# Long convolution and soft mixture of experts on one core: the second transform stage on four frequencies at once, one in each quarter of the matrix array

## The chip, the cores and the metric

The kernel runs on one core of a Trainium2 chip. The metric is device time in microseconds (us) from the first to the last instruction, the median of several runs. Every program here runs on one core. PE is TensorE's matrix array, DVE is VectorE, ACT is ScalarE, POOL is GpSimd, SP is the engine that issues the transfers.

## The reference

A causal convolution along the sequence, written as a Fourier transform of twice the length, and then a soft mixture of experts over all 45,568 rows:

```python
B, S, D = 8, 5696, 128
Xf = rfft(x, n=2*S, axis=1); Hf = rfft(h, n=2*S, axis=0)
y  = irfft(Xf * Hf, n=2*S, axis=1)[:, :S, :]
x  = y.reshape(B*S, D)
logits = x @ phi                               # phi: 128 x 32 slots
d = softmax over rows of logits;  slot_input = d.T @ x
slot_out = per expert: relu(slot_input @ w1) @ w2
out = softmax over slots of logits @ slot_out  # 45568 x 128, float32
```

## The kernel before

The transform is done in two stages, over 90 and over 64 points. Per batch (and once for the filter `h`, called batch 0) there are eight steps. Stage A does the 90-point transform and writes to HBM. Stage B reads 128 rows for a *unit* of two frequencies in each of two halves (23 units a batch): b1 is the 64-point transform, VectorE multiplies by the filter's spectrum, b2 transforms back. Stage C takes the result, folds it, makes the logits and the softmax sums. The three stages run interleaved, each for another batch: step 9 starts B for the filter, step 17 B for the first batch, step 26 starts C; stage A ends with step 71, B with step 80. A step has three *slots* of stage B, and each slot holds b1 of unit u and b2 of unit u-1.

```python
wt = fconst.tile([P, NP, P], F32, name="wt")     # NP = 45 tables of 128 x 128, block-diagonal
vt = fconst.tile([P, NP, P], F32, name="vt")
ps  = mid.enter_context(tc.tile_pool(name="ps", bufs=6, space=PSUM))   # bank() takes from here
aps = mid.enter_context(tc.tile_pool(name="aps", bufs=2, space=PSUM))

def stage_b1(u):
    g, i = divmod(u, NU); n = min(2, NP - 2 * i)
    t_ = gs.pop(u)
    p = bank()
    pv = p[:, :].rearrange("p (q c d) -> p q c d", c=2, d=D)
    for q in range(n):
        nc.tensor.matmul(p[:, q * 256:(q + 1) * 256], wt[:, 2 * i + q, :],
                         t_[:, q, :, :].rearrange("p c d -> p (c d)"), start=True, stop=True)
    # ... g == 0: the filter's spectrum Hr, Hi is made from pv; return
    for t, H in ((pr, Hr), (pi, Hi)):            # DVE, out of PSUM
        nc.vector.tensor_tensor(out=t[:, 0:n, :, :], in0=pv[:, 0:n, :, :], in1=H[...], op=AL.mult)
    # ... DVE: yf = pr[0] - pi[1], pr[1] + pi[0]; prods[u] = yf

def stage_b2(u):
    # ...
    p = bank()
    for q in range(n):
        nc.tensor.matmul(p[:, q * 256:(q + 1) * 256], vt[:, 2 * i + q, :], y_[:, q, :, :]..., ...)
    nc.scalar.activation(st[:, 0:n, :], p[:, 0:n * 256]..., AF.Copy)   # zst, then to HBM

def slot_b():
    if us:
        u = us.pop(0); prefetch(u + AHEAD)
        stage_b1(u); wait_b2.append(u)
        if len(wait_b2) > 1: stage_b2(wait_b2.pop(0))
    elif wait_b2: stage_b2(wait_b2.pop(0))

# one step t (C works on pairs of steps):
#   stage_a(t, 0); [odd: dispatch]; slot_b(); [even: C1, C4]; [odd: C2 transposes, C6]; slot_b()
#   [even: fold_out, C5]; stage_a(t, 1); [odd: C3 = logits and their maximum mx]; slot_b(); ...
```

Everything is float32: a matmul becomes two matrix instructions (the trace has 810 for the 405 matmuls of b1). The tile layer makes all waits from the program's order, and for PSUM it orders any two accesses to one bank of one tile in which one engine writes.

## Time and profile before

| | before |
|---|---|
| time, median of 4 runs | 1061.7 us |
| profiled run | 1066.3 us |
| busy share PE, DVE, ACT, POOL | 91, 68, 48, 34% |
| start of steps 17, 26; of C's pairs 23 and 27 (steps 72 and 80) | 111, 196; 804, 894 us |
| eight steps in the steady part (steps 34 to 66) | 104.9 us |

Starts of steps are those of stage A's first matmul of the step in the trace. How its lines are read is shown in the prediction. The short way: the slices say where PE is full, the chain of waits says which engine's instructions stand one behind the other up to the end, and the groups give for each line the count, the mean duration and what ended the idle time before it.

### The profile page before, as it was taken

Reading aid. Unit: us, or ns where it says so; the run is one execution under the profiler, and the core shown is the slowest. Engines: PE = TensorE matmul, PEld = TensorE weight load, DVE = VectorE, ACT = ScalarE, POOL = GpSimd, SP = SyncE. Lnnn points to the kernel's source line nnn. Section 1 sums busy time; section 2 is a strip of 40 time slices with the busy share of each in tenths; the row PEclk is TensorE's granted clock in tenths of the full one; section 3 lists DMA queues with packets and bytes.
Section 4 is the critical chain, followed back from the end, with each engine's and each line's share of the span. In section 5 each row is a group of like instructions: output and inputs, shape, how many; then the busy total and the mean of one; then the engine's idle time right before and its main releaser. Section 6 shows DMA issues by size and latency. Waiting matters only on the chain.

```text
span 1066.3 us, 17253 instructions
## 1 busy us (share of the span) xinstructions
PE 968.4 (91%) x5690; PEld 606.3 (57%) x5690; DVE 723.7 (68%) x1384; ACT 517.1 (48%) x1049; POOL 358.5 (34%) x340
## 2 busy tenths in 40 slices
PE   6688899999999999999999999999998998775983
PEld 2255566555666666666666566656665555343683
DVE  2044566677777787777777777777778888565442
ACT  3467444455555555555555555555553434343342
POOL 5523222323433343334333333343321212384000
PEclk9899999999999999999999999999999999886855
DMA  6999999988888889888988898889877777953398
GB/s 193 288 277 289 304 333 283 296 257 258 245 274 260 265 236 282 263 257 244 279 254 270 238 276 265 259 241 278 285 214 245 247 229 214 242 158 156 135 406 340
DMA packets 175111, 275.50 MB, mean 258 GB/s; under 512 B 12864, under 2 KB 115776, under 8 KB 169263
## 3 DMA queue, kind: packets, MB, share of 16 engines
q1 hardware_dynamic: 174447, 274.04, 82.8%
q8 instruction: 47, 0.77, 0.3%
q10 hardware_dynamic: 576, 0.36, 0.1%
q14 instruction: 41, 0.34, 0.1%
HBM read 145.95 MB, written 128.39 MB: 257 GB/s over the span
## 4 chain that ended last, share of the span: by engine, by line
PE 64%; DVE 21%; DMA 8%; issue 2%; ACT 2%; POOL 1%; SPq 0%; DVEq 0%; ACTq 0%; POOLq 0%
PE bank L190 18%; PE bank L220 12%; PE bank L308 11%; PE bank L256 11%; DVE yf L242 5%; DMA out_dram<-o 4%; PE bank L338 3%; DVE pr L238 3%; DMA gt<-f 3%; DVE pi L238 3%; PE bank L348 2%; DVE y L325 2%; DVE y L324 2%; PE bank L377 2%; DVE yf L244 2%
## 5 line engine op out<-in xcount | busy, mean ns | idle before, releaser
L179 POOL TENSOR_TENSOR x<-xc 128x512 f32<-128x512 f32 x144 | 187.5, 1303 | 281.9 <-PE bank L190 237.0
L190 PE MATMUL bank<-x,s 128*128 128x512 f32 x576 | 270.6, 597 | 8.1 <-POOL x L179 8.1
L259 ACT ACTIVATE zst<-bank 128x512 f32<-128x512 f32 (+1 forms) x184 | 108.2, 588 | 296.3 <-PE bank L256 280.6
L220 PE MATMUL bank<-gt,wt 128*128 128x256 f32 x810 | 220.4, 395 | 20.1 <-DMA gt<-f 19.8
L220 PEld LDWEIGHTS bank<-gt,wt 128*128 128x128 f32 x810 | 145.4, 192 | 115.1 <-issue 54.3
L256 PE MATMUL bank<-yf,vt 128*128 128x256 f32 x720 | 189.4, 385 | 17.7 <-DVE yf L244 12.5
L192 ACT ACTIVATE fst<-bank 128x512 f32<-128x512 f32 x288 | 168.5, 598 | 67.7 <-PE bank L190 53.1
L238 DVE TENSOR_TENSOR pr<-bank,Hr 128x512 f32<-128x512 f32 (+1 forms) x184 | 124.6, 677 | 97.8 <-PE bank L220 97.7
L256 PEld LDWEIGHTS bank<-yf,vt 128*128 128x128 f32 x720 | 133.5, 190 | 53.0 <-issue 13.8
L190 PEld LDWEIGHTS bank<-x,s 128*128 128x128 f32 x576 | 107.5, 192 | 94.6 <-issue 61.8
L308 PE MATMUL bank<-zc,i 128*64 128x512 f32 x480 | 120.3, 612 | 3.5 <-DMA zc<-z 3.5
L238 DVE TENSOR_TENSOR pi<-bank,Hi 128x512 f32<-128x512 f32 (+1 forms) x184 | 123.0, 668 | 0.0
L242 DVE TENSOR_TENSOR yf<-pr,pi 128x256 f32<-128x256 f32 (+1 forms) x184 | 113.5, 617 | 6.4
L338 PE MATMUL bank<-ident,y 128*128 128x128 f32 x512 | 67.2, 289 | 15.3 <-DVE y L325 15.3
L358 DVE TENSOR_REDUCE mx<-lt 64x1 f32<-64x360 f32 x64 | 33.2, 518 | 70.1 <-ACT lt L352 69.7
L244 DVE TENSOR_TENSOR yf<-pr,pi 128x256 f32<-128x256 f32 (+1 forms) x184 | 76.5, 416 | 0.0
L338 PEld LDWEIGHTS bank<-ident,y 128*128 128x128 f32 x512 | 62.2, 150 | 20.6 <-issue 16.5
L339 ACT ACTIVATE yt<-bank 128x360 f32<-128x360 f32 x128 | 56.4, 471 | 35.6 <-PE bank L338 35.6
L229 DVE SCALAR_TENSOR_TENSOR Hr<-bank,turn,pr 128x128 f32<-128x128 f32 x45 | 15.7, 348 | 75.6 <-ACT pr L227 75.6
L324 POOL TENSOR_TENSOR y<-y,op 128x512 f32<-128x512 f32 x32 | 38.4, 1200 | 80.9 <-DVE op L313 80.9
L308 PEld LDWEIGHTS bank<-zc,i 128*64 128x64 f32 x480 | 30.1, 137 | 56.3 <-issue 53.9
L413 POOL TENSOR_TENSOR L<-L,rs 128x512 f32<-128x512 f32 x32 | 33.6, 1051 | 77.8 <-DVE rs L412 64.7
(97 smaller groups left out, 922.2 us busy)
## 6 DMA issues: line engine op xcount, KB each, us to landing
f<-fst SPq DMA_DIRECT2D x144, 360.0 KB
gt<-f SPq DMA_DIRECT2D x198, 256.0 KB
z<-zst SPq DMA_DIRECT2D x176, 256.0 KB
zc<-z SPq DMA_DIRECT2D x60, 720.0 KB
xc<-in_x_dram SPq DMA_DIRECT2D x64, 320.0 KB
out_dram<-o SPq DMA_DIRECT2D x16, 1024.0 KB
out_dram<-o SPq DMA_DIRECT2D x8, 768.0 KB
c_t<-cst SPq DMA_DIRECT2D x26, 180.0 KB
```

What stands on the lines that cost most here:

```text
L179: nc.gpsimd.tensor_tensor(out=y_[:, :, :], in0=t_[:, 0, :, :], in1=t_[:, 1, ::-1, :], op=AL.subtract if comp else AL.add)
L190: nc.tensor.matmul(p[:, :], s1[:, tab[G], :], src[:, :, :].rearrange("p n d -> p (n d)"), start=True, stop=True)
L192: nc.scalar.activation(st[:, :, G, :], p[:, :].rearrange("p (n d) -> p n d", d=D), AF.Copy)
L220: nc.tensor.matmul(p[:, q * 256:(q + 1) * 256], wt[:, 2 * i + q, :], t_[:, q, :, :].rearrange("p c d -> p (c d)"), start=True, stop=True)
L238: nc.vector.tensor_tensor(out=t[:, 0:n, :, :], in0=pv[:, 0:n, :, :], in1=H[:, 2 * i:2 * i + n, :].unsqueeze(2).broadcast_to([P, n, 2, D]), ...
L242: nc.vector.tensor_tensor(out=y_[:, 0:n, 0, :], in0=pr[:, 0:n, 0, :], in1=pi[:, 0:n, 1, :], op=AL.subtract)
L244: nc.vector.tensor_tensor(out=y_[:, 0:n, 1, :], in0=pr[:, 0:n, 1, :], in1=pi[:, 0:n, 0, :], op=AL.add)
L256: nc.tensor.matmul(p[:, q * 256:(q + 1) * 256], vt[:, 2 * i + q, :], y_[:, q, :, :].rearrange("p c d -> p (c d)"), start=True, stop=True)
L259: nc.scalar.activation(st[:, 0:n, :], p[:, 0:n * 256].rearrange("p (q c) -> p q c", q=n), AF.Copy)
L308: nc.tensor.matmul(p[h_ * HP:(h_ + 1) * HP, :], i1[:, tab, :], t_[:, o, :, q, :], start=True, stop=True)
L324: eng.tensor_tensor(out=part(v, 1), in0=part(v, 0), in1=o_[:, :, :], op=AL.subtract)
L338: nc.tensor.transpose(p[:, i * P:(i + 1) * P], ys[T][:, k * CH + i, 0:D], ident[:, :])
```

## The change

The tables `wt` and `vt` held two 64 x 64 blocks on the diagonal of a 128 x 128 block, the rest zeros. The change stores the 64 x 64 blocks alone and lets four frequencies use the four quarters of the array at once: the row half is the half of the frequencies for b1, the column half is the frequency's parity; b2 goes the other way. The change has the instructions of different row halves write to different banks, so a unit's output is spread over two banks. To use no more than the eight banks of the kernel before (6 + 2), b1 of unit u and b2 of unit u-1 share one tile of two banks: b1 has columns 0 to 255 of both, b2 columns 256 to 511. Stage A's write to HBM is split in two, as its rows now lie in two groups of partitions.

```diff
-    ps = mid.enter_context(tc.tile_pool(name="ps", bufs=6, space=PSUM))
-    aps = mid.enter_context(tc.tile_pool(name="aps", bufs=2, space=PSUM))
+    rings = [mid.enter_context(tc.tile_pool(name="ps", bufs=4, space=PSUM))]
+    bps = front.enter_context(tc.tile_pool(name="bps", bufs=2, space=PSUM))
-    wt = fconst.tile([P, NP, P], F32, name="wt")
-    vt = fconst.tile([P, NP, P], F32, name="vt")
+    wt = fconst.tile([P, NP, HP], F32, name="wt")
+    vt = fconst.tile([P, NU, 2, HP], F32, name="vt")
 ...
-        p = bank()
-        for q in range(n):
-            nc.tensor.matmul(p[:, q * 256:(q + 1) * 256], wt[:, 2 * i + q, :], ...)
+        for a in range(2):
+            r = slice(a * HP, (a + 1) * HP)
+            for q in range(n):
+                nc.tensor.matmul(bt[q * HP:(q + 1) * HP, a, 0:2 * D], wt[r, 2 * i + q, :],
+                                 t_[r, q, :, :].rearrange("p c d -> p (c d)"), ...)
 ...
-        p = bank()
         for q in range(n):
-            nc.tensor.matmul(p[:, q * 256:(q + 1) * 256], vt[:, 2 * i + q, :], ...)
+            r = slice(q * HP, (q + 1) * HP)
+            for a in range(2):
+                nc.tensor.matmul(bt[a * HP:(a + 1) * HP, q, 2 * D:4 * D], vt[r, i, a, :], ...)
 ...
         def slot_b():
+            bt = bps.tile([P, 2, 512], F32, name="bt", tag="bt")
+            fresh = bool(us)
+            if fresh:
                 u = us.pop(0)
                 prefetch(u + AHEAD)
-                stage_b1(u)
+                stage_b1(u, bt)
                 wait_b2.append(u)
-                if len(wait_b2) > 1:
-                    stage_b2(wait_b2.pop(0))
+            if len(wait_b2) > fresh:
+                stage_b2(wait_b2.pop(0), bt)
```

(Cut: the tables, the filter's branch, the split write, the loads, the early return of `slot_b` when nothing is left to do, and the branch of `slot_b` that this replaces. The layouts of the data follow. P is 128, HP 64, D 128, NP 45, NU 23.)

More of the change, by code (lines that the diff above doesn't have):

```diff
@@ L15, with transform_tables @@
 PSUM = bass.MemoryType.PSUM
-def transform_tables(S, N1, N2, CH, Z0, X0, F0):
+def transform_tables(S, N1, N2, CH, Z0, X0, F0, F1):
     N, R1, HALF, P = N1 * N2, S // N2, N2 // 2, 2 * N2
@@ L36, in transform_tables @@
     i1 = np.stack([np.cos(a0), -np.sin(a0), -np.cos(a0)], 1)
-    s1 = np.pad(s1, [(X0, P - R1 - X0), (0, 0), (F0, P - N1 - F0)])
+    NP = N1 // 2
+    part = s1
+    s1 = np.zeros((P, 3, P))
+    for a, p in enumerate((F0, F1)):
+        s1[X0:X0 + R1, :, p:p + NP] = part[:, :, a * NP:(a + 1) * NP]
     i1 = np.pad(i1[np.arange(N1).reshape(2, N1 // 2).T.reshape(-1)],
@@ L44, in transform_tables @@
     w = np.concatenate([np.cos(a2), np.sin(a2)], 1)
-    NP = N1 // 2
     back = np.arange(N2).reshape(2, HALF // CH, CH).transpose(1, 0, 2).reshape(-1)
-    wbd = np.zeros((2 * N2, NP, 2 * N2))
-    vbd = np.zeros((2 * N2, NP, 2 * N2))
-    for par in range(2):
-        r = slice(par * N2, (par + 1) * N2)
-        wbd[par::2, :, r] = w[par * NP:(par + 1) * NP].transpose(1, 0, 2)
-        vbd[r, :, r] = w[par * NP:(par + 1) * NP][:, back].transpose(2, 0, 1)
-    turn = (N1 - 1) / 2 * alpha[:, None] + (N2 - 1) / 2 * omega
-    tn = np.zeros((2 * N2, 2, NP))
-    for par in range(2):
-        r = slice(par * N2, (par + 1) * N2)
-        tn[r, 0] = np.cos(turn[par * NP:(par + 1) * NP]).T / N
-        tn[r, 1] = np.sin(turn[par * NP:(par + 1) * NP]).T / N
-    return [np.ascontiguousarray(t, dtype=np.float32) for t in (s1, i1, wbd, vbd, tn)]
+    NU = (NP + 1) // 2
+    turn = (N1 - 1) / 2 * alpha[:, None] + (N2 - 1) / 2 * omega
+    wq = np.zeros((2, N2, NP, N2))
+    vq = np.zeros((2, N2, NU, 2, N2))
+    tn = np.zeros((2, N2, 2, NU, 2))
+    for a in range(2):
+        wq[a] = w[a * NP:(a + 1) * NP].transpose(1, 0, 2)
+        for q in range(NP):
+            vq[q % 2, :, q // 2, a] = w[a * NP + q][back].T
+            tn[q % 2, :, 0, q // 2, a] = np.cos(turn[a * NP + q]) / N
+            tn[q % 2, :, 1, q // 2, a] = np.sin(turn[a * NP + q]) / N
+    wq, vq, tn = [t.reshape(P, *t.shape[2:]) for t in (wq, vq, tn)]
+    return [np.ascontiguousarray(t, dtype=np.float32) for t in (s1, i1, wq, vq, tn)]
 @with_exitstack
@@ L106 @@
     SPLIT = R1 // 16 * 16
-    Z0, X0, F0 = 20, 20, 19
+    Z0, X0, F0, F1 = 20, 20, 6, 82
     ctx.enter_context(tc.manual_schedule())
@@ L111 @@
         nc.inline_tensor(t, f"tab_{n}").ap()
-        for n, t in zip(("s1", "i1", "w", "v", "turn"), transform_tables(S, N1, N2, CH, Z0, X0, F0))]
-    fd = [nc.dram_tensor(f"f_{g}", (N2, N1, 2, D), F32, kind="Internal").ap() for g in range(B + 1)]
+        for n, t in zip(("s1", "i1", "w", "v", "turn"), transform_tables(S, N1, N2, CH, Z0, X0, F0, F1))]
+    fd = [nc.dram_tensor(f"f_{g}", (2, N2, NP, 2, D), F32, kind="Internal").ap() for g in range(B + 1)]
     zd = [nc.dram_tensor(f"z_{b}", (NP, 2 * N2, 2, D), F32, kind="Internal").ap() for b in range(B)]
@@ L130 @@
     ypool = work.enter_context(tc.tile_pool(name="ypool", bufs=1))
+    front = ExitStack()
     mid, inner, cload = ExitStack(), ExitStack(), ExitStack()
-    ps = mid.enter_context(tc.tile_pool(name="ps", bufs=6, space=PSUM))
-    aps = mid.enter_context(tc.tile_pool(name="aps", bufs=2, space=PSUM))
-    front = ExitStack()
+    rings = [mid.enter_context(tc.tile_pool(name="ps", bufs=4, space=PSUM))]
+    bps = front.enter_context(tc.tile_pool(name="bps", bufs=2, space=PSUM))
     fconst = front.enter_context(tc.tile_pool(name="fconst", bufs=1))
@@ L140 @@
     s1 = apool.tile([P, 3, P], F32, name="s1", tag="s1", bufs=1)
-    wt = fconst.tile([P, NP, P], F32, name="wt")
-    vt = fconst.tile([P, NP, P], F32, name="vt")
-    turn = fconst.tile([P, 2, NP], F32, name="turn")
-    Hr = fconst.tile([P, NP, D], F32, name="Hr")
-    Hi = fconst.tile([P, NP, D], F32, name="Hi")
+    wt = fconst.tile([P, NP, HP], F32, name="wt")
+    vt = fconst.tile([P, NU, 2, HP], F32, name="vt")
+    turn = fconst.tile([P, 2, NU, 2], F32, name="turn")
+    Hr = fconst.tile([P, NU, 2, D], F32, name="Hr")
+    Hi = fconst.tile([P, NU, 2, D], F32, name="Hi")
     def bank():
-        return ps.tile([P, 512], F32, name="bank", tag="bank")
+        rings.append(rings.pop(0))
+        return rings[-1].tile([P, 512], F32, name="bank", tag="bank")
     xs = {}
@@ L194, in stage_a @@
         n0 = comp * HALF + CH * j
-        nc.sync.dma_start(out=fd[g][n0:n0 + CH, :, :, :].rearrange("n k g d -> k n (g d)"),
-                          in_=st[F0:F0 + N1, :, :, :].rearrange("k n g d -> k n (g d)"))
+        for a, p in enumerate((F0, F1)):
+            nc.sync.dma_start(
+                out=fd[g][a, n0:n0 + CH, :, :, :].rearrange("n q c d -> q n (c d)"),
+                in_=st[p:p + NP, :, :, :].rearrange("k n c d -> k n (c d)"))
     gs, prods = {}, {}
@@ L208, in load_g, with stage_b1 @@
             out=t_[:, 0:n, :, :].rearrange("p q c d -> p (q c d)"),
-            in_=fd[g].rearrange("r (a p) c d -> (r a) (p c d)",
-                                a=2)[:, 4 * i * D:(4 * i + 2 * n) * D])
+            in_=fd[g].rearrange("a r q c d -> (a r) (q c d)")[:, 4 * i * D:(4 * i + 2 * n) * D])
         gs[u] = t_
-    def stage_b1(u):
+    def stage_b1(u, bt):
         g, i = divmod(u, NU)
@@ L216, in stage_b1 @@
         t_ = gs.pop(u)
-        p = bank()
-        pv = p[:, :].rearrange("p (q c d) -> p q c d", c=2, d=D)
-        for q in range(n):
-            nc.tensor.matmul(p[:, q * 256:(q + 1) * 256], wt[:, 2 * i + q, :],
-                             t_[:, q, :, :].rearrange("p c d -> p (c d)"), start=True, stop=True)
+        for a in range(2):
+            r = slice(a * HP, (a + 1) * HP)
+            for q in range(n):
+                nc.tensor.matmul(bt[q * HP:(q + 1) * HP, a, 0:2 * D], wt[r, 2 * i + q, :],
+                                 t_[r, q, :, :].rearrange("p c d -> p (c d)"),
+                                 start=True, stop=True)
+        r = slice(0, n * HP)
+        pv = bt[r, :, 0:2 * D].rearrange("p a (c d) -> p a c d", c=2)
         if g == 0:
-            for q in range(n):
-                m = 2 * i + q
+            for a in range(2):
                 pr = bpool.tile([P, 2, D], F32, name="pr", tag="pr")
                 for c in range(2):
-                    nc.scalar.activation(pr[:, c, :], pv[:, q, c, :], AF.Copy,
-                                         scale=turn[:, 0, m:m + 1])
+                    nc.scalar.activation(pr[r, c, :], pv[:, a, c, :], AF.Copy,
+                                         scale=turn[r, 0, i, a:a + 1])
                 nc.vector.scalar_tensor_tensor(
-                    out=Hr[:, m, :], in0=pv[:, q, 1, :], scalar=turn[:, 1, m:m + 1],
-                    in1=pr[:, 0, :], op0=AL.mult, op1=AL.add)
+                    out=Hr[r, i, a, :], in0=pv[:, a, 1, :], scalar=turn[r, 1, i, a:a + 1],
+                    in1=pr[r, 0, :], op0=AL.mult, op1=AL.add)
                 nc.vector.scalar_tensor_tensor(
-                    out=Hi[:, m, :], in0=pv[:, q, 0, :], scalar=turn[:, 1, m:m + 1],
-                    in1=pr[:, 1, :], op0=AL.mult, op1=AL.subtract, reverse1=True)
+                    out=Hi[r, i, a, :], in0=pv[:, a, 0, :], scalar=turn[r, 1, i, a:a + 1],
+                    in1=pr[r, 1, :], op0=AL.mult, op1=AL.subtract, reverse1=True)
             return
@@ L238, in stage_b1, with stage_b2 @@
             nc.vector.tensor_tensor(
-                out=t[:, 0:n, :, :], in0=pv[:, 0:n, :, :],
-                in1=H[:, 2 * i:2 * i + n, :].unsqueeze(2).broadcast_to([P, n, 2, D]), op=AL.mult)
+                out=t[r, :, :, :], in0=pv,
+                in1=H[r, i, :, :].unsqueeze(2).broadcast_to([n * HP, 2, 2, D]), op=AL.mult)
         y_ = bpool.tile([P, 2, 2, D], F32, name="yf", tag="yf")
-        nc.vector.tensor_tensor(out=y_[:, 0:n, 0, :], in0=pr[:, 0:n, 0, :], in1=pi[:, 0:n, 1, :],
+        nc.vector.tensor_tensor(out=y_[r, :, 0, :], in0=pr[r, :, 0, :], in1=pi[r, :, 1, :],
                                 op=AL.subtract)
-        nc.vector.tensor_tensor(out=y_[:, 0:n, 1, :], in0=pr[:, 0:n, 1, :], in1=pi[:, 0:n, 0, :],
+        nc.vector.tensor_tensor(out=y_[r, :, 1, :], in0=pr[r, :, 1, :], in1=pi[r, :, 0, :],
                                 op=AL.add)
         prods[u] = y_
-    def stage_b2(u):
+    def stage_b2(u, bt):
         g, i = divmod(u, NU)
@@ L253, in stage_b2 @@
         y_ = prods.pop(u)
-        p = bank()
         for q in range(n):
-            nc.tensor.matmul(p[:, q * 256:(q + 1) * 256], vt[:, 2 * i + q, :],
-                             y_[:, q, :, :].rearrange("p c d -> p (c d)"), start=True, stop=True)
+            r = slice(q * HP, (q + 1) * HP)
+            for a in range(2):
+                nc.tensor.matmul(bt[a * HP:(a + 1) * HP, q, 2 * D:4 * D], vt[r, i, a, :],
+                                 y_[r, a, :, :].rearrange("p c d -> p (c d)"),
+                                 start=True, stop=True)
         st = bpool.tile([P, 2, 2 * D], F32, name="zst", tag="zst", bufs=3)
-        nc.scalar.activation(st[:, 0:n, :], p[:, 0:n * 256].rearrange("p (q c) -> p q c", q=n),
-                             AF.Copy)
+        nc.scalar.activation(st[:, 0:n, :], bt[:, 0:n, 2 * D:4 * D], AF.Copy)
         nc.sync.dma_start(
@@ L417, in dispatch @@
     def dispatch(T):
-        ap_ = aps.tile([P, 512], F32, name="ap", tag="ap")
+        ap_ = bank()
         d_ = ds.pop(T)
@@ L541, in slot_b @@
         def slot_b():
-            if us:
+            if not us and not wait_b2:
+                return
+            bt = bps.tile([P, 2, 512], F32, name="bt", tag="bt")
+            fresh = bool(us)
+            if fresh:
                 u = us.pop(0)
                 prefetch(u + AHEAD)
-                stage_b1(u)
+                stage_b1(u, bt)
                 wait_b2.append(u)
-                if len(wait_b2) > 1:
-                    stage_b2(wait_b2.pop(0))
-            elif wait_b2:
-                stage_b2(wait_b2.pop(0))
-        for tab, src, first in ((wt, t_w, LAG_B - 2), (vt, t_v, LAG_B + NJ - 2)):
-            p0 = 2 * PER * (t - first)
-            if 0 <= p0 < NP:
-                p1 = min(NP, p0 + 2 * PER)
-                nc.sync.dma_start(out=tab[:, p0:p1, :], in_=src[:, p0:p1, :])
+            if len(wait_b2) > fresh:
+                stage_b2(wait_b2.pop(0), bt)
+        for tab, src, first, n, k in ((wt, t_w, LAG_B - 2, NP, 2 * PER),
+                                      (vt, t_v, LAG_B + NJ - 2, NU, PER)):
+            p0 = k * (t - first)
+            if 0 <= p0 < n:
+                v = slice(p0, min(n, p0 + k))
+                nc.sync.dma_start(out=tab[:, v], in_=src[:, v])
         if pair(1 - 2 * ahead) is not None:
@@ L603 @@
             front.close()
+            rings.append(mid.enter_context(tc.tile_pool(name="ps2", bufs=4, space=PSUM)))
             last = work.enter_context(tc.tile_pool(name="last", bufs=1))
@@ L677 @@
                 out=hidT[:, g, k0:k0 + 4, :], in_=p[:, :].rearrange("p (k c) -> p k c", k=4))
-    sop = aps.tile([P, 512], F32, name="ap", tag="ap")
+    sop = bank()
     for g in range(EG):
```

## The prediction

> **What bounds the kernel now.** I read the page first: busy times, slices, chain of waits, groups.
>
> ```profile
> PE 968.4 (91%) x5690; PEld 606.3 (57%) x5690; DVE 723.7 (68%) x1384; ACT 517.1 (48%) x1049; POOL 358.5 (34%) x340
> ...
> PEclk9899999999999999999999999999999999886855
> DMA  6999999988888889888988898889877777953398
> ...
> PE 64%; DVE 21%; DMA 8%; issue 2%; ACT 2%; POOL 1%; SPq 0%; DVEq 0%; ACTq 0%; POOLq 0%
> ...
> L220 PE MATMUL bank<-gt,wt 128*128 128x256 f32 x810 | 220.4, 395 | 20.1 <-DMA gt<-f 19.8
> ...
> L256 PE MATMUL bank<-yf,vt 128*128 128x256 f32 x720 | 189.4, 385 | 17.7 <-DVE yf L244 12.5
> ```
>
> The matrix engine leads and owns the chain. L220 (first half of stage two, "b1") and L256 (second half, "b2") are 24% of the chain. Next I asked for busy time by stretches of 100 us (columns: PE, PEld, DVE, ACT, POOL, clock, DMA share, GB/s).
>
> ```profile
> 300.00:400.00 100.00, 99.54 (x560) 61.93 (x559) 79.52 (x148) 53.07 (x103) 38.20 (x35) 1.00 0.87 261
> 800.00:900.00 100.00, 88.99 (x555) 55.82 (x555) 83.45 (x169) 40.84 (x82) 19.80 (x22) 1.00 0.75 236
> ```
>
> From 200 to 800 us PE has no free time (99.5%); VectorE at 79% and DMA at 87% are close behind. Then I read single slots in the order of time; a slot is one b1 and the previous unit's b2.
>
> ```profile
> 161.95 1.03 PE L220 MATMUL bank<-gt,wt 128*128 128x256 f32 x4
> ...
> 162.81 1.03 PE L256 MATMUL bank<-yf,vt 128*128 128x256 f32 x4
> 163.02 0.69 DVE L238 TENSOR_TENSOR pr<-bank,Hr 128x512 f32<-128x512 f32 x1 [1.36 <-PE bank L220]
> ...
> 163.62 0.68 DVE L238 TENSOR_TENSOR pi<-bank,Hi 128x512 f32<-128x512 f32 x1
> 163.68 1.03 PE L220 MATMUL bank<-gt,wt 128*128 128x256 f32 x4
> ```
>
> b1 issues for 0.86 us (161.95 to 162.81), b2 for 0.87 (to 163.68): 1.72 us a slot, four 128x256 matrix instructions of 0.214 us each per half. The 1.03 includes a 0.17 us tail that overlaps the next. The point to see: b2 starts at 162.81, **before** VectorE begins pr on b1's result, because they use different banks.
>
> **What the Trainium skill says.** "TensorEngine Tiling (Array Packing)", Key Properties: tiles run in parallel, and changing the tiling mode drains the engine. The trace agrees: eight 128x32 instructions of 360 columns (L348) go from 403.04 to 403.85 in the timeline, against 8 x 0.30 = 2.4 us one after another, so four run at once; going from L256 to the two-tile L308 takes 0.96 us start to start where 0.85 is work, so a switch costs some 0.11. "PSUM — Partial Sum Buffer", PSUM bank collisions raise a hardware error: two engines must not touch one bank and quadrant at once, disjoint columns or not. Nothing in the trace of before shows this; the changed program's waits do. "TensorE: Matmul & The Clock Gate", Part 1: the matrix clock is halved after an idle window of about 3.4 us. The trace agrees and is stricter; these are single windows:
>
> ```profile
> 105.18:108.59 3.41, 1.77 (x7) 0.76 (x5) 1.46 (x5) 2.67 (x9) 1.27 (x1) 1.00 0.84 244
> 112.01:115.42 3.41, 1.47 (x6) 0.68 (x4) 0.31 (x2) 1.62 (x4) 1.59 (x2) 1.00 1.02 335
> 115.42:118.83 3.41, 3.15 (x8) 1.91 (x7) 2.71 (x6) 0.00 (x0) 0.00 (x0) 0.50 1.03 329
> ```
>
> A window with 1.77 us busy left the clock alone; one with 1.47 us (1.94 us idle) was followed by a window at 0.50. So idle of some 1.9 us within one window costs a half-speed window.
>
> **The change part by part.**
>
> Removed: each full unit had 2 x 4 instructions over the whole array. It now has 2 x 8 on quarters, four at once: two rounds of 0.214 = 0.43 us per half. Taken alone, a slot goes from 1.72 to 0.86 us. There are 207 b1 and 184 b2, so some 160 us of PE time is removed. The tables halve (2.9 MB less of 275 MB).
>
> Added, small: stage one's write is split in two (144 issues more, same bytes, 1 KB pieces as before); the mode changes before b1 and after b2, 0.11 us each, 0.22 per slot, of which 4 of 12 per two steps were paid already; the general ring of banks is 4 rather than 6 plus 2.
>
> Added, large: b1(u) and b2(u-1) now share one two-bank tile, b1 in columns 0 to 255 of both banks and b2 in 256 to 511. In program order VectorE's pr(u) and pi(u) stand between them. I resolved the waits of the built program: in before, the first matmul of b2 waits for yf of the *previous* unit and an old bank; in after, it waits for pi of *this* unit, every slot. So the order becomes b1, pr, pi, b2, with PE idle between. From the slot above: b1's issue ends at 162.81; tail and signal 0.21 until pr starts (163.02); pr and pi 1.28 (until 164.30); from VectorE's end to the first matmul of b2 0.14 (yf ends 846.83, L256 starts 846.97). Gap 0.21 + 1.28 + 0.14 = 1.63 us.
>
> New slot: 0.43 + 1.63 + 0.43 + 0.22 = 2.71 us against 1.72: **+0.99**. Not hidden, as PE is in order and had no free time.
>
> One slot in six is worse. In odd steps the reduction mx and its followers come before the third slot's pr in VectorE's order:
>
> ```profile
> 404.43 1.05 DVE L358 TENSOR_REDUCE mx<-lt 64x1 f32<-64x360 f32 x2 [1.78 <-ACT lt L352]
> 405.51 0.16 DVE L363 SCALAR_TENSOR_TENSOR low<-mx,low 128x1 f32<-128x1 f32 x1
> 405.71 0.16 DVE L366 TENSOR_TENSOR df<-low 128x1 f32<-128x1 f32 x1
> 405.78 0.68 DVE L238 TENSOR_TENSOR pr<-bank,Hr 128x512 f32<-128x512 f32 x1
> ```
>
> They take 1.35 us and begin 1.39 after the logits matmul's start (403.04); b1's result would be ready 1.35 after it. So this slot waits 1.4 us more. The other slots' VectorE backlog fits in PE's work between slots, while stage one runs.
>
> The sum by stretches (steps 17 to 25, A and B alone, at 116 to 200 us; steps 26 to 71, all stages, to 803 us; steps 72 to 80 without stage one, to 905 us):
> - Until 116 us: PE waits for DMA there; smaller tables: -4.
> - Steps 17 to 25: 26 slots x 0.99 = 26, less 5 of idle time that it had: +20.
> - Steps 26 to 71: eight steps take 104.84 us now (L308 in the chain at 304.38 and 409.22). Added per eight: 23 x 0.99 = 22.8, - 1.8 for switches paid already, + 4 x 1.4 = 5.6: 26.6. Times 46/8: +153.
> - Steps 72 to 80: VectorE bound, some 22.7 us per two steps; the new serial chain is 8.6 (other PE work) + 0.5 + 6 x 2.6 + 2.7 of backlog = 27.4: +20.
> - Clock: the slot behind mx leaves PE idle about 2.8 us, more than 1.9; wherever the windows fall, some 70% of these 23 slots start one or two half-speed windows, each costing 1.5 us: about +40, and +15 in the stretches where slots stand next to each other.
> - After 905 us: nothing.
>
> 1062 - 4 + 20 + 153 + 20 + 55 = **1306 us**.
>
> **The rivals.**
> 1. *The packing pays.* If b2 didn't wait, PE would need 160 - 35 us less, VectorE (82 us per 105) and DMA (91 per 105) would bind instead, and it would end near 980. For: PE at 99.5%. Against: the wait is in the program, for every unit that has a b2.
> 2. *The quarters do not overlap four ways* with these row and column halves: 0.43 us more per half, up to +160, near 1440. Against: four row strips (L716) and four column strips (L348) each overlapped fully.
> 3. *The clock stays up*, as matmuls are still busy 70% of the time: near 1250.
> 4. *The ring of 4 banks or the doubled writes bind.* The queue has only eight transfers in flight, but each step gets longer, so its load falls; I give these nothing.
>
> **Range and chances.** 1250 without the clock, 1306 with my guess, up to 1385 if many windows run at half speed; an overestimated gap gives 1225. Range 1225 to 1385. Faster 0.03, same 0.02, slower 0.95.
>
> **What would show it right or wrong.** Right: b2's row of waits names VectorE's pi, some 180 times and 1.4 us or more each (250 us in all); PE's busy share falls from 91% to about 65 to 70%; ACT's zst comes right behind each pi; clock below 1.00 in 200 to 800 us; DMA share falls below 0.75. Each half takes 0.43 + 0.17 us as a group of eight. Wrong: b2 starting before pi ends, which would mean rival 1; b1 taking 0.86 for eight, rival 2; clock 1.00 throughout, rival 3.

## The result

| | before | after |
|---|---|---|
| time, median | 1061.7 us | 1300.1 us |
| range, 4 runs each | 1060.0 to 1063.7 | 1296.5 to 1305.4 |
| ratio | | 1.225 (95%: 1.220 to 1.230) |
| busy share of PE, DVE | 91, 68% | 72, 54% |
| mean matrix clock | 0.953 | 0.911 |
| eight steps in the steady part | 104.9 us | 136.2 us |

A ratio is the mean time of one kernel's runs over that of the other's of the same rounds, so it is not quite the ratio of the medians. The changed kernel is 22% slower.

The page of the changed kernel, the lines that answer to those of before (busy times; the clock and DMA rows of the 40 slices; the chain of waits by engine; the two halves of stage B, now lines 266 and 227):

```profile
PE 937.9 (72%) x7220; PEld 418.2 (32%) x7220; DVE 701.3 (54%) x1386; ACT 522.6 (40%) x1051; POOL 355.4 (27%) x340
...
PEclk9898997998999899989999899999999788888775
DMA  7888777776677667766677767667665566477199
...
PE 61%; DVE 25%; DMA 7%; issue 2%; ACT 2%; SPq 1%; POOL 0%; DVEq 0%; ACTq 0%; POOLq 0%
...
L266 PE MATMUL bt<-yf,vt 64*64 64x256 f32 x1440 | 133.8, 437 | 289.3 <-DVE pi L247 289.3
...
L227 PE MATMUL bt<-gt,wt 64*64 64x256 f32 x1620 | 142.6, 418 | 21.2 <-DMA gt<-f 9.9
```

The two halves of stage B did become shorter: 134 + 143 us busy, from 189 + 220. But L266 carries 289 us of idle PE time ahead of it, all of it ended by VectorE's pi. PE's own list of waits has it as one row (us in total, times, longest):

```profile
PE bt L266 <- DVE pi L247: 289.3, 176, 3.0
```

One slot of the changed kernel in the order of time, PE and VectorE:

```profile
502.35 0.66 PE L227 MATMUL bt<-gt,wt 64*64 64x256 f32 x8
...
503.08 0.69 DVE L247 TENSOR_TENSOR pr<-bt,Hr 128x512 f32<-128x512 f32 x1 [4.03 <-PE bt L227]
503.69 0.68 DVE L247 TENSOR_TENSOR pi<-bt,Hi 128x512 f32<-128x512 f32 x1
...
504.40 0.43 DVE L251 TENSOR_TENSOR yf<-pr,pi 128x256 f32<-128x256 f32 x1
...
504.42 0.66 PE L266 MATMUL bt<-yf,vt 64*64 64x256 f32 x8 [1.41 <-DVE pi L247]
```

Eight instructions of b1 take 0.66 us as a group, tail included: four quarters do run at once. Then PE stands still until pi has ended (504.37). Before, b2 began ahead of pr. What b2 reads is the *previous* unit's yf, which was ready long before; the yf at 504.40 is for the next slot. So b2 waits for no data: it waits because pi reads the bank that b2 is about to write.

The third slot of an odd step, where the logits' maximum mx stands ahead of pr on VectorE:

```profile
529.49 0.81 PE L358 MATMUL bank<-yt,phi 128*32 128x360 f32 x8
...
530.23 0.66 PE L227 MATMUL bt<-gt,wt 64*64 64x256 f32 x8
...
530.88 1.05 DVE L368 TENSOR_REDUCE mx<-lt 64x1 f32<-64x360 f32 x2 [3.16 <-ACT lt L362]
...
532.24 0.69 DVE L247 TENSOR_TENSOR pr<-bt,Hr 128x512 f32<-128x512 f32 x1
...
533.57 0.66 PE L266 MATMUL bt<-yf,vt 64*64 64x256 f32 x8 [2.68 <-DVE pi L247]
```

From b1 to b2 3.34 us, against 2.07 in the slot above. Two single windows (us, then busy PE, PEld, DVE, ACT, POOL, clock, DMA share, GB/s) show what such a gap does to the clock:

```profile
494.73:498.14 3.41, 0.90 (x13) 0.21 (x8) 2.45 (x6) 0.67 (x2) 0.98 (x1) 1.00 0.98 259
498.14:501.56 3.42, 3.26 (x11) 1.47 (x12) 0.87 (x3) 0.68 (x2) 0.00 (x0) 0.50 0.94 312
```

PE was busy for 0.90 us of the first, and the next one ran at half speed. Summed over the trace, the clock stood at one half for 74 us between steps 26 and 71, against none before.

Where the 237 us (profiled runs) came from: 1.5 until step 17, 32 in steps 17 to 25, 178 in steps 26 to 71, 29 from the start of step 72 to the start of step 80, and -3 after that.

### The profile page after: what moved, and what is told of

It is laid out like the page before. It is cut to its first block, busy times and chain, and to the rows that moved or that the text cites. A ratio compares the mean times of both kernels' runs of the same rounds, so it can differ in the third digit from the quotient of the medians.

```text
span 1303.6 us, 20188 instructions
## 1 busy us (share of the span) xinstructions
PE 937.9 (72%) x7220; PEld 418.2 (32%) x7220; DVE 701.3 (54%) x1386; ACT 522.6 (40%) x1051; POOL 355.4 (27%) x340
## 4 chain that ended last, share of the span: by engine, by line
PE 61%; DVE 25%; DMA 7%; issue 2%; ACT 2%; SPq 1%; POOL 0%; DVEq 0%; ACTq 0%; POOLq 0%
PE bank L196 20%; PE bt L266 10%; PE bank L318 9%; DVE pr L247 9%; DVE pi L247 8%; PE bt L227 8%; PE bank L348 5%; DMA out_dram<-o 3%; DVE mx L368 2%; PE bank L434 2%; PE bank L358 2%; DMA gt<-f 1%; PE bank L387 1%; ACT lt L362 1%; PE bank L410 1%
## 5 line engine op out<-in xcount | busy, mean ns | idle before, releaser
L266 PE MATMUL bt<-yf,vt 64*64 64x256 f32 x1440 | 133.8, 437 | 289.3 <-DVE pi L247 289.3
L196 PE MATMUL bank<-x,s 128*128 128x512 f32 x576 | 315.7, 679 | 10.2 <-DMA xc<-in_h_dram 8.3
L270 ACT ACTIVATE zst<-bt 128x512 f32<-128x512 f32 (+1 forms) x184 | 108.2, 588 | 480.1 <-PE bt L266 396.8
L247 DVE TENSOR_TENSOR pr<-bt,Hr 128x512 f32<-128x512 f32 (+1 forms) x184 | 127.0, 690 | 281.9 <-PE bt L227 281.9
L266 PEld LDWEIGHTS bt<-yf,vt 64*64 64x64 f32 x1440 | 40.4, 140 | 379.4 <-DVE pi L247 373.8
L227 PE MATMUL bt<-gt,wt 64*64 64x256 f32 x1620 | 142.6, 418 | 21.2 <-DMA gt<-f 9.9
L247 DVE TENSOR_TENSOR pi<-bt,Hi 128x512 f32<-128x512 f32 (+1 forms) x184 | 125.2, 681 | 0.0
L227 PEld LDWEIGHTS bt<-gt,wt 64*64 64x64 f32 x1620 | 46.4, 137 | 143.3 <-issue 91.1
L251 DVE TENSOR_TENSOR yf<-pr,pi 128x256 f32<-128x256 f32 (+1 forms) x184 | 79.7, 433 | 6.4
L253 DVE TENSOR_TENSOR yf<-pr,pi 128x256 f32<-128x256 f32 (+1 forms) x184 | 76.8, 418 | 0.0
L395 POOL MEMSET dt<- 64x8 f32 x32 | 3.4, 106 | 225.2 <-ACT dn L398 130.7
L323 DVE TENSOR_TENSOR y<-bank,y 128x512 f32<-128x512 f32 x32 | 22.1, 691 | 62.5 <-PE bank L318 62.5
```

The lines of the kernel that those rows point to most:

```text
L196: nc.tensor.matmul(p[:, :], s1[:, tab[G], :], src[:, :, :].rearrange("p n d -> p (n d)"), start=True, stop=True)
L227: nc.tensor.matmul(bt[q * HP:(q + 1) * HP, a, 0:2 * D], wt[r, 2 * i + q, :], t_[r, q, :, :].rearrange("p c d -> p (c d)"), start=True, sto ...
L247: nc.vector.tensor_tensor(out=t[r, :, :, :], in0=pv, in1=H[r, i, :, :].unsqueeze(2).broadcast_to([n * HP, 2, 2, D]), op=AL.mult)
L251: nc.vector.tensor_tensor(out=y_[r, :, 0, :], in0=pr[r, :, 0, :], in1=pi[r, :, 1, :], op=AL.subtract)
L253: nc.vector.tensor_tensor(out=y_[r, :, 1, :], in0=pr[r, :, 1, :], in1=pi[r, :, 0, :], op=AL.add)
L266: nc.tensor.matmul(bt[a * HP:(a + 1) * HP, q, 2 * D:4 * D], vt[r, i, a, :], y_[r, a, :, :].rearrange("p c d -> p (c d)"), start=True, stop ...
```

## The experiments

**Theory.** The shared bank makes b2 wait for VectorE's reading of b1 in every slot; packing itself works. **Rival A:** the packing is dear (mode switches, quarter tiles, twice the instructions). **Rival B:** the smaller ring of banks or the doubled writes cost the time. All kernels gave correct results, and each was timed in three rounds against the kernel before.

| run | what it is | median us | ratio to before (95%) | eight steps, us (steps 34 to 66) |
|---|---|---|---|---|
| shared_alone | before + shared banks | 1348.7 | 1.269 (1.263 to 1.276) | 143.3 |
| own_banks | after, own banks | 1090.0 | 1.025 (1.018 to 1.032) | 104.1 |
| both_first | after, readers last | 1094.7 | 1.031 (1.023 to 1.038) | 106.7 |
| ring4_split | before + ring of 4, split writes | 1108.3 | 1.043 (1.037 to 1.048) | 104.8 |
| own_banks2 | own_banks, filter's batch mended | 1061.7 | 0.998 (0.995 to 1.002) | 104.1 |
| ring4_split2 | ring4_split, the same mended | 1067.2 | 1.004 (1.000 to 1.009) | 104.8 |
| after_warm | after, gap filled with idle matmuls | 1265.2 | 1.189 (1.185 to 1.193) | 130.7 |
| after_c3late | after, mx behind the slot | 1237.1 | 1.162 (1.157 to 1.166) | 125.7 |
| own_lag2 | own_banks2, b2 two units behind | 1018.3 | 0.958 (0.954 to 0.962) | 96.5 |
| own_lag2_c3 | own_lag2, mx behind the slot | 998.7 | 0.940 (0.935 to 0.945) | 95.5 |
| before_lag2_c3 | before with both orders, 4 load buffers | 1091.2 | 1.027 (1.021 to 1.033) | 109.5 |
| before_lag2_c3b | the same, 5 load buffers | 1044.5 | 0.983 (0.979 to 0.987) | 103.7 |

**shared_alone.** The kernel before with one part of the change alone (and with it the general ring of 4 banks, cut here; ring4_split2 below shows that this part costs next to nothing).

```diff
-        p = bank()                       # in b1 and in b2
+    # bt: [P, 2, 512]; b1 of q in bt[:, q, 0:256], b2 of q in bt[:, q, 256:512]
-                stage_b1(u)
+                bt = bps.tile([P, 2, 512], F32, name="bt", tag="bt")
+                stage_b1(u, bt)
 ...
-                    stage_b2(wait_b2.pop(0))
+                    stage_b2(wait_b2.pop(0), bt)
```

> The kernel before with one part of the change alone: b1(u) and b2(u-1) share one tile of two banks, in the program order of the change; matmuls stay over the whole array, tables and writes stay, ring of 4. Theory: each of 184 slots gains the gap of 1.63 us that I worked out, +300 us, and some 50 us more from the slot behind mx and half-speed windows: near 1400 us (1340 to 1450). Rival A (packing dear, sharing free): near 1062.

Measured 1349 us, in the range but near its lower end. The clock stood at one half for only 17 us in steps 26 to 71; what else fell short of the 1400 was not looked into. PE's list of waits has the same row as the changed kernel:

```profile
PE bt L255 <- DVE pi L238: 263.5, 176, 2.5
```

Eight steps grew by 143.3 - 104.9 = 38.4 us, on average 1.67 for each of 23 slots, the slots behind mx included. In an ordinary slot of this trace b2 starts 2.52 us after b1 (600.76 and 603.28), 0.86 of it work: a gap of 1.66, where 1.63 was worked out beforehand. So sharing alone, without any packing, costs more than the whole change does; the packing gives back 49 us of it.

**own_banks.** The changed kernel with two tiles of two banks in one buffer each, as many banks as before.

```diff
-    bps = front.enter_context(tc.tile_pool(name="bps", bufs=2, space=PSUM))
+    bps = front.enter_context(tc.tile_pool(name="bps", bufs=1, space=PSUM))
-            bt = bps.tile([P, 2, 512], F32, name="bt", tag="bt")
-                stage_b1(u, bt)
+                stage_b1(u, bps.tile([P, 2, 512], F32, name="bt", tag="bt"))
-                stage_b2(wait_b2.pop(0), bt)
+                stage_b2(wait_b2.pop(0), bps.tile([P, 2, 512], F32, name="b2", tag="b2"))
```

> The changed kernel, but b1 and b2 write to two tiles of two banks each (one buffer apiece), so as many banks as before; packing, tables, split writes and the ring of 4 stay. b2 then waits for yf of the unit before, as in the kernel before. Theory (the shared banks cost the time): the row of b2 waiting for VectorE's pi (289 us, 176 times) disappears, and with PE freed of some 125 us the end comes near 985 us (950 to 1020), bound by VectorE, DMA and PE together. Rival A (the packing itself, its mode switches and quarter tiles, is dear): it stays above 1200. Rival B (the small ring and the doubled writes): it stays above 1200.

The row that waits for pi is gone, and 210 of the 238 us went with it: rival A falls. But the expected 985 us were missed by 105. Two things were open: the filter's batch (steps 9 to 16) took 98 us instead of 69, and the steady part, with a third less busy PE time in stage B, took 104.1 us per eight steps as if nothing had been saved. They are taken up below.

**both_first.** The changed kernel, the same banks shared, only the order in a slot changed (diff shortened).

```diff
-                stage_b1(u, bt)          # matmuls of b1, then pr, pi
+                mm_b1(u, bt)             # matmuls alone
                 wait_b2.append(u)
-            if len(wait_b2) > fresh:
-                stage_b2(wait_b2.pop(0), bt)
+            old = wait_b2.pop(0) if len(wait_b2) > fresh else None
+            if old is not None: mm_b2(old, bt)
+            if fresh: stage_b1(u, bt)    # pr, pi, yf
+            if old is not None: stage_b2(old, bt)   # zst
```

> The changed kernel with the same shared tile of two banks, only the order within a slot changed: all matmuls of b1(u) and b2(u-1) first, then the readers. Same instructions, same banks. Theory (it is the order of reader and writer in a shared bank): PE's wait for pi disappears; instead VectorE's pr starts 0.43 us later in each slot and ScalarE's zst comes after pi. Near 1010 us (970 to 1070). If sharing a bank is dear in itself, whatever the order, it stays near 1300.

1095 us: PE no longer waits for pi, with the bank still shared. So 205 of the 238 us are the price of writer, reader, writer in one bank, in that order. It missed its range (970 to 1070). The filter's batch is not the reason here (67 us); the steady part took 106.7 us per eight steps and steps 72 to 79 took 102 us, before 90. PE now waits for the previous yf, and VectorE's pr for b2, the second writer of its bank:

```profile
PE bt L270 <- DVE yf L257: 88.4, 74, 2.9
...
DVE pr L251 <- PE bt L270: 111.7, 107, 3.2
```

own_banks2 below, where pr need not wait for b2, is 33 us faster. So even in the better order the shared bank does not seem to be free; no run separates this further.

**ring4_split.** The kernel before with the small parts of the change.

```diff
-    ps = ... bufs=6;  aps = ... bufs=2
+    rings = [... bufs=4];  bps = ... bufs=1     # tags "bt" and "b2", two banks each
-        nc.sync.dma_start(out=fd[g][n0:n0 + CH, :, :, :]..., in_=st[F0:F0 + N1, ...]...)
+        for k0 in (0, NP):
+            nc.sync.dma_start(out=fd[g][n0:n0 + CH, k0:k0 + NP, :, :]..., in_=st[F0 + k0:F0 + k0 + NP, ...]...)
```

> The kernel before with the small parts of the change alone: a general ring of 4 banks, b1 and b2 in their own two-bank tiles, and stage one's write in two issues. Theory: within 2% of before (1045 to 1080). Rival B (small ring and doubled writes cost the time): a good part of the 240 us shows, above 1150.

4% slower, outside the range, though far from rival B's 1150. The starts of the steps say where: step 9 to step 17 took 111 us, before 69; afterwards eight steps take 104.8 as before. In the filter's batch there is no b2, so my single b1 tile left two of four banks unused, and each b1 waited for its own readers. This was a flaw of the experiment, shared with own_banks. Mended in both:

```diff
-    bps.tile([P, 2, 512], F32, name="bt", tag="bt")
+    bps.tile([P, 2, 512], F32, name="bt", tag="b2" if u < NU and u % 2 else "bt")
```

**ring4_split2**

> ring4_split with the same mending. If the 46 us that ring4_split lost came from the single pair of banks in the filter's batch (its steps 9 to 16 took 111 us, before 69), it returns to before within 2% (1050 to 1080), and the ring of 4 and the doubled writes are free. If they cost it, it stays near 1105.

1067 us, 0.4% over before and at most 0.9% by the interval: the smaller ring and the doubled writes cost next to nothing, rival B falls.

**own_banks2**

> own_banks with one flaw mended: in the first batch (the filter), which has no b2, b1 now alternates between both pairs of banks; with one pair it waited for its own readers, and steps 9 to 16 took 98 us instead of 67. If that is the whole of it, 30 us go there, the steady part stays at 104 us per eight steps, and the end is near 1060 us (1045 to 1070): the same as before, with PE some 88% busy. If the loss of own_banks came from elsewhere (the packing, the writes), it stays near 1090.

1062 us, as expected. With the wait gone and nothing else wrong, the packing gives nothing at all (0.998), although PE's busy time fell from 968 to 877 us in the profiled runs (91 and 83%, tails counted). The gain was lost in a new wait, for which PE's list has this row:

```profile
PE b L266 <- DVE yf L253: 53.2, 62, 1.2
```

One such place in the order of time:

```profile
502.76 1.98 PE L196 MATMUL bank<-x,s 128*128 128x512 f32 x4
...
504.88 1.26 POOL L185 TENSOR_TENSOR x<-xc 128x512 f32<-128x512 f32 x1 [2.39 <-PE bank L196]
505.06 1.37 DVE L251 TENSOR_TENSOR yf<-pr,pi 128x256 f32<-128x256 f32 x1
...
505.13 0.66 PE L227 MATMUL bt<-gt,wt 64*64 64x256 f32 x8 [0.38 <-PE bank L196]
...
506.36 0.41 DVE L253 TENSOR_TENSOR yf<-pr,pi 128x256 f32<-128x256 f32 x1
...
506.91 0.66 PE L266 MATMUL b<-yf,vt 64*64 64x256 f32 x8 [1.12 <-DVE yf L253]
```

PE arrives at b2 early and waits for yf. VectorE is 84% busy now and in order, so PE can't run ahead of it by more than one unit. And yf took 1.37 us where it takes 0.42 alone: it runs beside GpSimd's sum of 504.88. Pairing each yf record with the GpSimd sums that overlap it by more than 0.15 us: alone it takes 0.42 us on average; overlapped it took 1.01 us (64 times) before, 1.24 us (83 times) in own_banks2, and only 5 were overlapped in the changed kernel. So VectorE loses some 83 x 0.82 = 68 us to this now, 38 before. The Trainium skill, "SBUF — State Buffer", Who interferes with whom, says that a VectorE instruction with two SBUF inputs contends with GpSimd's reads; the trace agrees for yf (two SBUF inputs), and pr and pi (one input in PSUM) stay at 0.67 to 0.69 us on average in all kernels. No run took GpSimd's sums away, so the size of this loss is read from the trace, not tested. By itself it did not keep the gain away: the next run has more of it.

**own_lag2.** If PE and VectorE wait for each other in turn, more distance between b1 and b2 must help; if VectorE's work or DMA is the bound, it can't.

```diff
-        y_ = bpool.tile([P, 2, 2, D], F32, name="yf", tag="yf")
+        y_ = bpool.tile([P, 2, 2, D], F32, name="yf", tag="yf", bufs=3)
-            if len(wait_b2) > fresh:
+            while len(wait_b2) > (2 if fresh else 0):
```

> own_banks2 with b2 two units behind b1 instead of one (yf in three buffers). Theory 1 for why 160 us less of matrix work gave nothing in the steady part (104.1 us per eight steps against 104.85): PE and VectorE, both in order, wait for each other in turn within a slot (PE waits 53 us for yf in own_banks). Then the wait goes and eight steps take some 96 us: end near 1010 us (985 to 1035). Theory 2: VectorE's own work, lengthened where GpSimd runs beside it, or the DMA is the bound: it stays within 1% of own_banks2, near 1060.

1018 us, as theory 1 has it: PE's wait for yf has gone from the list, and eight steps fell from 104.1 to 96.5 us. b2's longest remaining row is small:

```profile
PE b L266 <- ACT zst L270: 7.4, 10, 0.8
```

Even more yf were overlapped by GpSimd than in own_banks2 (99, 1.21 us on average, a loss of some 78 us), and still the kernel was 43 us faster. So it was the distance of one unit that held own_banks2 back; VectorE's lengthened work by itself left room for 1018 us.

**own_lag2_c3** then lets the logits and mx go behind the third slot:

```diff
-        if pair(1) is not None:
-            stage_c3(pair(1))
         slot_b()
+        if pair(1) is not None:
+            stage_c3(pair(1))
```

> own_lag2, and the logits matmul and its reduction mx moved behind the third slot of odd steps, so VectorE does not stand idle for the logits with pr waiting behind mx (98 us of waiting for lt in the changed kernel, 69 in own_banks). Theory 1: a further 1 to 2 us per two steps, near 985 us (960 to 1025). Theory 2: no change, near 1060.

999 us, 6% faster than before, and better than both kernels. The steady part did not give what was expected of it (1 to 2 us per two steps): it gave 1.0 per eight. Of the 16 us between the profiled runs of own_lag2 and this one, 9 lie in steps 72 to 79. In a stretch of 100 us of its steady part PE, VectorE and DMA are all close to full:

```profile
500.00:600.00 100.00, 95.14 (x797) 45.02 (x797) 91.68 (x160) 57.97 (x113) 41.97 (x38) 1.00 0.95 282
```

**before_lag2_c3.** Is it the order alone? The kernel before with the same two changes of order. Its full-size tables left no room for a third yf, so I took a load buffer away (five to four).

> The kernel before, unpacked, with the two changes of order of own_lag2_c3 (b2 two units behind, logits behind the third slot); its full-size tables leave no room, so the loads ahead go from five buffers to four. Theory (PE is full at 99.5%, so only less matrix work helps, and the order changes help only together with the packing): 1055 to 1070 us. Rival (the order changes alone made the 6% of own_lag2_c3): near 1000.

1091 us, out of the range upwards, and the cause is my buffer: PE now waits for the loads.

```profile
PE bank L220 <- DMA gt<-f: 55.4, 30, 9.3
```

It decides little, so it was done again without that flaw. **before_lag2_c3b** issues b2 between the matmuls and the readers of b1, which needs no third yf:

```diff
-                stage_b1(u)
+                stage_b1(u, wait_b2.pop(0) if len(wait_b2) > 1 else None)   # stage_b2(old) after b1's matmuls
                 wait_b2.append(u)
-                if len(wait_b2) > 1:
-                    stage_b2(wait_b2.pop(0))
```

> before_lag2_c3 without its flaw: it had one load buffer fewer, and PE waited 55 us for those loads. Here b2 of two units ago is issued between the matmuls and the readers of b1, so yf needs no third buffer and all five load buffers stay; everything else as in the kernel before. Theory (unpacked, PE is full, so the order changes alone give nothing): 1050 to 1070 us, eight steps at 104 to 105 us. Rival (the order alone gives the gain of own_lag2_c3): near 1000 us, eight steps near 96.

1045 us: 1.7% faster than before (the interval leaves out 1), and more than expected (1050 to 1070). Of the 25 us between the profiled runs, 2 lie before step 17, 6 in steps 17 to 25, 7 in steps 72 to 79 and 8 after the start of step 80 (there the clock stood at one half for 68 us, before 87). Steps 26 to 71 gave only 2: in the steady part (same columns as above) PE is full and the order can't help:

```profile
500.00:600.00 100.00, 100.00 (x533) 61.61 (x535) 79.19 (x148) 53.76 (x105) 36.47 (x34) 1.00 0.88 269
```

So neither part does it alone: packing gives 0.2%, the order 1.7%, both together 6.0%.

**after_warm** tests the term for the clock. It does *more* work: two matmuls that nobody reads, in the gap behind mx.

```diff
+        if warm:                          # third slot of odd steps, between b1 and b2
+            for c0, c1 in ((0, 512), (0, 256)):
+                nc.tensor.matmul(bank()[:, 0:c1], ident[:, :], y_[...][:, c0:c1], start=True, stop=True)
```

> The changed kernel with idle time filled: in the third slot of odd steps, where PE waits 2.7 us (behind mx), two matmuls of 1.28 us in all, whose result nobody reads, stand between b1 and b2. They lengthen nothing, as PE waits there anyway. Theory (that wait triggers half-speed windows; the changed kernel has 74 us of them in steps 26 to 71 and more later, each costing at most half its length): those windows go and the end is some 35 us earlier, near 1265 us (1250 to 1285), although PE does more work. Rival: the half-speed windows cost nothing: 1300 within 1%.

1265 us, as expected: 35 us earlier. The mean clock rose from 0.911 to 0.949, and eight steps fell from 136.2 to 130.7. That leaves 130.7 - 104.9 = 25.8 us per eight steps for the waits, where the prediction's sum had 26.6.

**after_c3late** tests the term for mx, in the changed kernel itself, with the same edit as own_lag2_c3.

> The changed kernel with the logits matmul and mx moved behind the third slot of odd steps. My sum had 1.4 us per two steps for pr standing behind mx there: 32 times gives -45 us, and with the long gap the half-speed windows it triggers go too, some -35 us: near 1220 us (1200 to 1245). If the reduction only delays the next slot instead, no gain: near 1300.

1237 us, 63 us less, inside the range. Against after_warm eight steps fell by another 5.1 us, 1.27 per two steps; the prediction had 1.4. (Both have no half-speed clock left in steps 26 to 71.)

## Why the prediction was right

The prediction said 1306 us, the kernel took 1300. By its own steps:

- *The gap.* Predicted 0.43 + 1.63 = 2.06 us from b1's start to b2's start; the slot shown took 2.07, and PE waited 289 us in 176 slots. shared_alone measured the gap by itself, own_banks and both_first took it away. This is shown. (The waits show that the tile layer keeps the engines apart in a bank; no run here tests what the chip would do without them.)
- *Four quarters at once.* Eight instructions in 0.66 us, tail included; predicted 0.60. Rival 2 of the prediction is out.
- *Switches of mode.* Predicted 0.11 each. In the changed kernel, A to b1 costs 512.49 to 514.31 in the timeline, 1.82 us for 1.71 of work: 0.11; from b2 to stage C's two-tile matmul 0.59 for 0.43: 0.16. Slightly low.
- *The slot behind mx.* Predicted 1.4 us, read off 1.27 in the trace (3.34 - 2.07), 1.27 by experiment.
- *The clock.* Predicted 55 us in all, 40 of it in steps 26 to 71. after_warm gave 35 by filling only the gap behind mx, 31 of it (profiled runs) in steps 26 to 71, where the 74 us of half-speed clock went to none. So the term was too large there, 40 for 31; some half-speed windows remained in steps 17 to 25 and after step 72.
- *By stretches,* with the clock's share: until step 17 predicted -4, measured +1.5 (1.6 us were gained in steps 9 to 16, but step 9 began 3.1 later; with the split writes and the full tables, in ring4_split2, it began 2.1 later, so the writes may cost something there; not tested further); steps 17 to 25: predicted 20 and part of the 15 for the clock, measured 32; steps 26 to 71: predicted 153 + 40, measured 178; steps 72 to 80: predicted 20 and the rest of the 15, measured 29 up to the start of step 80. The terms are good to some 15 us, and that the sum came within 6 us of the result is in part luck: 193 for 178 was too much, and the other terms together were too little.
- *Small parts.* The ring and the writes were given nothing; ring4_split2 (0.4%, at most 0.9%) agrees.
- *A reading.* PE at 99.5% holds from 300 to 800 us; from 200 to 300 us it was 97.6%. No term rests on it.

One step of the prediction was wrong, though the result did not hang on it: rival 1, "it would end near 980" if b2 didn't wait. own_banks2 is that kernel, and it ended at 1062. The prediction subtracted 125 us of PE time and took VectorE's 82 us per eight steps as a floor that could be reached. It left out that PE and VectorE, both in order and one unit apart, cannot both be kept full: PE waited 53 us for yf. (VectorE's yf also grew beside GpSimd, but own_lag2 shows that this alone did not stop the gain.) One more unit of distance brought 43 us, and mx out of the way another 20, to 999 us.

The predicted PE share, 65 to 70%, was a little low (72%).

## What to carry to other kernels

When two results share a PSUM bank, look at the program's order of writer, reader and next writer in it: a matmul group that writes another column range of the bank waits for the readers of the first, and on an in-order engine that wait stands in full. Issue all writers of a bank ahead of its readers, or, better here by 33 us, give each its own bank, which needed no bank more. And when the full engine is made faster, ask at once what distance in units the next one allows: less matrix work paid nothing until b2 was moved one unit further behind.

## What the Trainium skill lacked or had wrong

- "TensorE: Matmul & The Clock Gate", Part 1, has the clock fall after an idle window of about 3.4 us (of shorter idle times it says, without a size, that they can make the clock swing). Here a window that was not idle was enough: 1.47 of 3.41 us busy (before) and 0.90 (after) were each followed by a window at 0.50, while 1.77 busy was not. Counted over the 14 traces in windows of 3.41 us: all 197 full-speed windows with at most 1.47 us of busy PE were followed by a half-speed one, 32 of the 130 with 1.48 to 1.9, and 16 of the 3693 above that, all of them later than 900 us. Gaps of 2.7 us cost 35 us in one run, which matmuls without use in them took away again.
- "TensorEngine Tiling (Array Packing)", Key Properties, names the drain at a change of mode without a size. Here 0.11 to 0.16 us per change.
- "TensorE: Matmul & The Clock Gate", Part 3, gives measured packings of 32-wide strips. Here 64 x 64 quarters in float32: two rounds of four instructions of 256 columns take 0.66 us with tail, against 1.03 us for four over the whole array that do the same work.
- "PSUM — Partial Sum Buffer", PSUM bank collisions raise a hardware error, tells what must be ordered, not what the order can cost when readers stand between two writers: here 1.66 us per slot, and a run 27% longer where this alone was done.
- "SBUF — State Buffer", Who interferes with whom, has no size for two-input VectorE instructions in float32: yf of 256 columns took 0.42 us alone and 1.24 us on average beside a GpSimd sum (own_banks2).
